# Six more blocks of layer 0's output projection folded to 448 rows, and the oT moves of layer 2 issued in five groups

## The chip, the cores and the metric

The kernel runs on one core of a Trainium2 chip. TensorE (PE in the profile) multiplies; VectorE (DVE) and ScalarE (ACT) do the elementwise work, empty the PSUM banks and normalise; SyncE (SP) issues nearly all the DMAs, in one queue and in program order; GpSimd (POOL) only fills a few tiles at the start. The metric is the device time of one execution in microseconds, the median of several runs.

## The reference

Four layers in a row on x of 2048 tokens x 448 values, in bfloat16. Layers 0 and 2 are windowed attention with 16 heads of 28 values, layers 1 and 3 a gated unit (GLU) with an inner width of 1792. The two attention layers have the same weights, and so have the two GLU layers.

```python
def _A_ref(x, wqkv, wo):          # H = 16, Dh = 28, W = 8, dil = 2
    ...
    idx = pos[:, None] - off[None, :]      # the token itself and 7 before it, two apart
    ...
    logits = jnp.einsum("bhsd,bhswd->bhsw", q, kg) * scale
    ...
    attn = _softmax(logits, axis=-1)
    o = jnp.einsum("bhsw,bhswd->bhsd", attn, vg)
    return o.transpose(0, 2, 1, 3).reshape(B, S, D) @ wo

def _B_ref(x, w_gate, w_up, w_down):
    h = (x @ w_gate) * (x @ w_up)
    return h @ w_down

x = A_x
x = x + _A_ref(_layernorm(x), A_wqkv, A_wo)
x = x + _B_ref(_layernorm(x), B_w_gate, B_w_up, B_w_down)
x = x + _A_ref(_layernorm(x), A_wqkv, A_wo)
x = x + _B_ref(_layernorm(x), B_w_gate, B_w_up, B_w_down)
```

What the change touches is the last step of `_A_ref`, the product of the attention's output o with wo.

## The kernel before

Tokens are tiled in 16 blocks of 128 (NBLK); x stays in SBUF as x_sb for the whole program. A layer is worked off in chunks of 256 or 512 tokens, and chunks of all four layers overlap in time, as dependencies allow.

Attention, for a chunk: bn_stats and xn (L583 to L604) normalise blocks of x; DMA transposes on SP (L607) turn xn_sb into xnTa; TensorE makes Q, K (WQK) and V (WV) from it. V is taken through a tile vt by plain DMAs (L723) and turned back by DMA transposes (L734) into v_sb, in windows of keys. The 17 query tiles (the first of 128 tokens, the others of 120; "query tile" 0 alone, then 1 and 2, 3 and 4 and so on as groups) go through a scores product (L837), exp and mask (L847, L854), and a weighted sum of V (L872) on 64*32 tiles of TensorE. L886 and L890 gather the sum in O_sb, L900 to L902 take the reciprocal of the softmax's denominator (a shuffle on VectorE, Ln and Exp on ScalarE), and the norm product L913 writes oT, the attention's output with head rows down the partitions.

oT has four chunks of 128 partitions: 4 groups of 32 rows, of which 28 are a head's values and 4 are padding. It is a ring over half of the tokens: 1024 columns. The output projection of two blocks B and B + 1 (`y_blocks`, key Y) multiplies oT's columns by wo_g, which is wo laid out in the same rows. TensorE works on 64 rows at a time with two such matmuls side by side (`twin_blocks`, `pair`, L352; L355 where a matmul is cut in four strips of 32 columns because it stands amid small-tile work). Unfolded that is 4 chunks x 2 halves x 2 blocks, 16 matmuls of 64 rows by 448 columns. Folded it is 14, for 448 rows instead of 512: the upper 64 rows of chunk 3 hold two heads, and four DMAs on SP (mv, L445, `oT<-oT`) copy these into the padding rows of the other chunks (table PADS: 3 or 4 rows deep, from and to the rows it names). The two blocks' lower halves of chunk 3 must then run side by side, so a fifth DMA (mw) copies the odd block's half from partitions 0 to 63 to 64 to 127; it waits for the four, and the projection waits for it. wo_g is brought into the same form by four DMAs from DRAM and one inside SBUF (wf, `wo_g<-in_A_wo_dram`, `wo_g<-wo_g`), once, after the last unfolded projection.

FOLD tells from which block on a layer is folded; `{0: 16, 2: 0}` is none in layer 0 and all in layer 2. There each pair of blocks has its own five moves: 8 x 5 = 40.

GLU, for a chunk: xn and transposes to xnTb, gate and up products (WGU, two PSUM banks side by side), g_sb from one bank by ScalarE (L979), hT = g_sb x the other bank by VectorE (L982), then the down product (WD). The last blocks' down product is at L994.

The order of all this isn't left to a queue at run time. Operations are given numbers, and tables ORDER (one list per engine) and BANKS (which PSUM bank a TensorE operation writes) fix what follows what on each engine; "538+539+556*349" in the TensorE list interleaves small-tile work with the wide matmuls. A semaphore wait is placed where an operation needs another engine's result. SP's list is an order of issue: a DMA whose data isn't ready holds all that stand behind it on SP. The tables were made by a search off line, with a model of durations.

Of the kernel before, what the change touches and what calls it, by code (L numbers as in the profile page):

```python
# [33 lines left out]
FOLD = {0: 16, 2: 0}  # L34
# [62 lines left out]
def grp_nc(g):  # L97
# [22 lines left out]
    ),  # L120
    "act": (
# [1003 lines left out]
```

## Time and profile before

| | us |
|---|---|
| runs | 381.83, 383.13, 384.85 |
| median | 383.13 |
| profiled execution | 383.47 |
| its span | 381.7 |

The rows of the page and the trace that the prediction uses are quoted there. How to read them: a row of the timeline has the start in us, the duration, the engine, the line, the operation, the tile written and the tiles read, the shape and how many instructions are put together; a bracket at the end tells how long the engine stood idle ahead of it and what ended that. "64*128" is the part of TensorE's array that a matmul uses, rows by columns; two of 64*128 run side by side. SPq is SP's queue: the time in which DMAs were being issued there, not the time of the transfers. An order's row, further down, has the line, the operation and the shape of the write's tile, and `x16` is that many in a row. Line numbers are one higher after the change up to L900, and three higher near the end.

### The profile page before, as it was taken

To read this page: it belongs to the slowest core of one execution; us is meant where nothing else is said; L and a number is where in the kernel's file an instruction comes from. 1 tells how busy PE (TensorE), PEld (TensorE's weight loads), DVE (VectorE), ACT (ScalarE), POOL (GpSimd) and SP (SyncE) were. 2 spreads that over 40 slices of the span, in tenths; PEclk is the share of its full clock that TensorE was granted. 3 is DMA by queue.
4 is the path that set the end of the run, shared out by engine and by line. 5 is a ranking of instruction groups with operands and counts; after the bars stand their busy time and mean duration, and the time that the engine had idled before them with its cause. 6 is when DMAs were issued, how large, how long until landed. Compare 5 with 4: busy or idle time off the path is not lost.

```text
span 381.7 us, 14424 instructions
## 1 busy us (share of the span) xinstructions
PE 373.9 (98%) x6388; PEld 209.8 (55%) x6388; DVE 288.1 (75%) x649; ACT 198.0 (52%) x379; POOL 7.8 (2%) x36
## 2 busy tenths in 40 slices
PE   7999999999999999999999999999989999999997
PEld 3645577654554445444676666555555544444864
DVE  7988999989759794968568977758887878266423
ACT  5798896766516355245645326628745633034410
POOL 7000000000000000000000000000000000000000
PEclk9999999999999999999999999999999999999999
DMA  7665543500130215332102221630124001502003
GB/s 262 165 158 147 96 127 81 97 7 3 26 78 16 43 25 72 43 43 44 34 18 27 45 50 29 106 47 6 25 43 76 9 19 29 122 17 47 2 2 120
DMA packets 56209, 22.97 MB, mean 60 GB/s; under 512 B 45812, under 2 KB 56132, under 8 KB 56148
## 3 DMA queue, kind: packets, MB, share of 16 engines
q1 hardware_dynamic: 56004, 22.00, 27.5%
q8 instruction: 50, 0.82, 0.9%
q14 instruction: 11, 0.09, 0.1%
q10 hardware_dynamic: 144, 0.06, 0.1%
HBM read 8.59 MB, written 2.71 MB: 30 GB/s over the span
## 4 chain that ended last, share of the span: by engine, by line
PE 91%; DVE 4%; ACT 2%; DMA 1%; issue 1%; SPq 0%; DVEq 0%
PE ps L352 82%; PE ps L355 4%; PE ps L837 2%; PE ps L872 2%; PE ps L994 1%; ACT qk L714 1%; DMA v_sb<-vt 1%; DVE xn_sb L604 1%; DVE st L583 1%; DMA x_sb<-in_A_x_dram 1%; DVE v_sb L806 0%; DVE WQK L522 0%; DVE hT L982 0%; DVE Qz L825 0%; DVE xnTa L628 0%
## 5 line engine op out<-in xcount | busy, mean ns | idle before, releaser
L352 PE MATMUL ps<-xnTb,WGU 64*128 64x512 bf16 (+1 forms) x1890 | 171.2, 332 | 0.3 <-DVE qk L714 0.3
L352 PEld LDWEIGHTS ps<-xnTb,WGU 64*128 64x128 bf16 x1890 | 92.3, 94 | 70.6 <-issue 1.6
L979 ACT ACTIVATE g_sb<-ps 128x512 bf16<-128x512 f32 (+1 forms) x140 | 69.3, 510 | 83.9 <-PE ps L352 72.0
L982 DVE TENSOR_TENSOR hT<-g_sb,ps 128x512 bf16<-128x512 bf16 (+1 forms) x140 | 78.0, 574 | 36.3 <-ACT g_sb L979 35.5
L352 PE MATMUL ps<-WD,hT 64*128 64x448 bf16 x794 | 81.3, 349 | 0.0
L352 PEld LDWEIGHTS ps<-WD,hT 64*128 64x128 bf16 x794 | 38.3, 94 | 33.3 <-ACT E_sb L847 0.4
L943 DVE TENSOR_TENSOR x_sb<-x_sb,ps 128x448 bf16<-128x448 bf16 x62 | 37.1, 613 | 21.6 <-PE ps L352 21.3
L352 PE MATMUL ps<-xnTa,WQK 64*128 64x512 bf16 (+1 forms) x490 | 51.8, 352 | 0.3 <-DVE WQK L522 0.2
L847 ACT ACTIVATE E_sb<-ps,shift_sb 128x1024 bf16<-128x1024 f32 (+1 forms) x36 | 37.5, 1072 | 12.0 <-PE ps L837 11.9
L583 DVE BATCH_NORM_STATS2 st<-x_sb 128x6 f32<-128x448 bf16 x64 | 38.3, 613 | 1.0 <-DMA x_sb<-in_A_x_dram 0.8
L604 DVE TENSOR_SCALAR xn_sb<-x_sb,mv,rstd 128x512 bf16<-128x512 bf16 (+1 forms) x64 | 35.4, 574 | 2.5 <-ACT rstd L588 2.0
L352 PEld LDWEIGHTS ps<-xnTa,WQK 64*128 64x128 bf16 x490 | 23.0, 94 | 20.7 <-DVE O_sb L890 0.4
L714 ACT ACTIVATE qk<-ps 128x1024 bf16<-128x1024 f32 (+1 forms) x29 | 26.6, 931 | 11.4 <-PE ps L352 6.3
L901 ACT ACTIVATE R_sb<-R_sb 128x480 f32<-128x480 f32 (+1 forms) x34 | 20.4, 604 | 17.2 <-DVE R_sb L900 17.0
L854 DVE TENSOR_TENSOR E_sb<-E_sb,MK 128x1024 bf16<-128x1024 bf16 (+1 forms) x36 | 23.5, 656 | 6.6 <-ACT E_sb L847 6.6
L352 PE MATMUL ps<-wo_g,oT 64*128 64x448 bf16 x236 | 27.1, 349 | 1.1 <-DVE hT L982 1.1
L913 DVE TENSOR_TENSOR oT<-O_sb,R_sb 128x480 bf16<-128x480 f32 (+3 forms) x36 | 21.9, 626 | 3.8 <-ACT R_sb L902 3.6
L352 PE MATMUL ps<-WV,xnTa 64*128 64x336 bf16 (+3 forms) x248 | 23.2, 304 | 0.5 <-DVE O_sb L890 0.5
L900 DVE STREAM_SHUFFLE R_sb<-O_sb 128x480 f32<-128x480 f32 (+1 forms) x34 | 23.1, 692 | 0.0
L586 ACT ACTIVATE lnv<-mv,eps_sb 128x2 f32<-128x2 f32 (+2 forms) x31 | 9.0, 295 | 25.9 <-DVE mv L585 24.0
L902 ACT ACTIVATE R_sb<-R_sb 128x480 f32<-128x480 f32 (+1 forms) x34 | 20.0, 607 | 0.3
L886 ACT ACTIVATE O_sb<-ps 128x512 f32<-128x512 f32 (+1 forms) x20 | 10.9, 570 | 15.8 <-PE ps L872 15.8
(66 smaller groups left out, 223.8 us busy)
## 6 DMA issues: line engine op xcount, KB each, us to landing
out_dram<-x_sb SPq DMA_DIRECT2D x15, 112.0 KB, 1.8
x_sb<-in_A_x_dram SPq DMA_DIRECT2D x3, 448.0 KB, 5.3
hT<-in_A_wqkv_dram SPq DMA_DIRECT2D x4, 224.0 KB, 4.4
WGU<-in_B_w_gate_dram SPq DMA_DIRECT2D x4, 224.0 KB, 3.9
WGU<-in_B_w_up_dram SPq DMA_DIRECT2D x4, 224.0 KB, 4.5
WD<-in_B_w_down_dram SPq DMA_DIRECT2D x2, 448.0 KB, 3.8
WGU<-in_B_w_gate_dram SPq DMA_DIRECT2D x2, 336.0 KB, 4.5
WGU<-in_B_w_up_dram SPq DMA_DIRECT2D x2, 336.0 KB, 4.8
```

The costliest lines, as they stand in the source:

```text
L352: return lambda E: E.matmul(out(), lhs(), rhs(), start=start, stop=stop)
L583: sc.add("dve", one(lambda E, B=B: E.bn_stats(st6[:, B, :], x_sb[:, B, :]), ("bn", li, B)), 525.0, deps=[("x", li - 1, B)] + ([("xn", li - ...
L604: sc.add("dve", one(lambda E, B=B, dst=dst, src=src: E.tensor_scalar(dst, src, mv[:, B, 0:1], rstd[:, B:B + 1], ALU.subtract, ALU.mult), ( ...
L714: return E.activation(dst, src, ACT.Copy) if hasattr(E, "activation") else E.tensor_copy(dst, src)
L847: return E.activation(E_sb[:, slot, 2 * hp:2 * hp + 2, 0:w], ps[:, b0:b0 + 2, 0:w], ACT.Exp, bias=shift_sb[:, 0:1], scale=SCALE)
L854: return E.tensor_tensor(e, e, MK[:, kind, 0:nc].unsqueeze(1).unsqueeze(1).to_broadcast([128, 2, w // nc, nc]), ALU.min)
L900: sc.add("dve", one(lambda E: E.stream_shuffle(R_sb[:, rs, 0:w], O_sb[:, os_, 0:w], [DH] * 32), ("Rs", li, qb)), dve_est(w) + 20.0, deps=[ ...
L901: sc.add("act", one(lambda E: E.activation(R_sb[:, rs, 0:w], R_sb[:, rs, 0:w], ACT.Ln), ("Rl", li, qb)), act_est(w, False), deps=[("Rs", l ...
L913: return E.tensor_tensor(oT[:, :, a % HALF:a % HALF + z - a], O[:, :, a - tok:z - tok], R_sb[:, rs, 0:w].rearrange("p (h n) -> p h n", h=4 ...
L943: sc.add("dve", one(lambda E: E.tensor_tensor(x_sb[:, B, :], x_sb[:, B, :], ps[:, bk[w], 0:D], ALU.add), ("x", li, B)), dve_est(D), deps=[ ...
L979: sc.add("act", one(lambda E, gs=gs, bk=bk: E.activation(g_sb[:, gs, 0:nt], ps[:, bk[0], 0:nt], ACT.Copy), ("G", li, j, fc)), act_est(nt), ...
L982: sc.add("dve", one(lambda E, gs=gs, bk=bk, fc=fc: E.tensor_tensor(hT[:, fc, hs, 0:nt], g_sb[:, gs, 0:nt], ps[:, bk[1], 0:nt], ALU.mult), ...
```

## The change

1. FOLD[0] goes from 16 to 10: layer 0's blocks 10 to 15, three pairs, are folded as well. The wf moves of the weights come after layer 0's projection of blocks 8 and 9 now, not after that of 14 and 15. Layer 0 has 3 x 5 moves of oT of its own.
2. GROUPS: in layer 0 each folded pair has its own five moves; in layer 2 there are five groups of blocks, 0 to 1, 2 to 5, 6 to 9, 10 to 13 and 14 to 15, with one set of five moves for each: 25. A set waits for the norms of all the group's blocks, and every projection of the group waits for its mw. The number of moves in all stays 40, and SP has 220 DMAs before and after.
3. The ring oT is shifted by 256 columns, so that a group's columns lie together; the norm product is cut where the ring wraps, at tokens 768 and 1792 instead of at 1024 (one instruction more in each attention layer).
4. ORDER and BANKS are new, for all engines.

```diff
-FOLD = {0: 16, 2: 0}
+FOLD = {0: 10, 2: 0}
+GROUPS = {0: tuple(range(0, 16, 2)), 2: (0, 2, 6, 10, 14)}
...
 ORDER = {
     "pe": (
-        "47 48 49 50 51 52 53 54 55 112 56 57 58 109 59 60 61 127 62 130 206 238 207 136 239 133 194 198 195 199 232 200 233 196 201 226 197 227 228 155 149 229 "
+        "47 48 49 50 51 52 53 54 55 112 56 57 58 59 109 60 61 62 206 130 127 207 238 133 136 239 198 194 232 195 233 196 200 199 197 201 228 226 155 149 227 229 "
...
-        cut = [tok] + [HALF] * (tok < HALF < tok + nq) + [tok + nq]
+        cut = [tok] + [e for e in range(HALF - 256, S, HALF) if tok < e < tok + nq] + [tok + nq]
...
-                return E.tensor_tensor(oT[:, :, a % HALF:a % HALF + z - a], ...
+                return E.tensor_tensor(oT[:, :, (a + 256) % HALF:(a + 256) % HALF + z - a], ...
...
     def y_blocks(li, B, prio):
         bk = Banks(2)
-        nd = []
-        for qb in range(NQB):
-            _, _, tok, nq = qb_info(qb)
-            if tok < 128 * (B + 2) and tok + nq > 128 * B:
-                nd.append(("N", li, qb))
+        def norms(b0, b1):
+            return [("N", li, qb) for qb in range(NQB) if qb_info(qb)[2] < 128 * b1 and qb_info(qb)[2] + qb_info(qb)[3] > 128 * b0]
+        nd = norms(B, B + 2)
         fold = B >= FOLD[li]
         if fold:
-            a = 128 * (B % 8)
-            for j, row, m, _, _ in PADS:
-                plain_dma("sp", oT[32 * j + DH:32 * j + 32, 0:m, a:a + 256], oT[row:row + 4 * m, 3, a:a + 256], ("mv", li, B, j), f"d_m{li}_{B}", deps=nd, prio=prio - 0.1)
-            plain_dma("sp", oT[64:128, 3, a + 128:a + 256], oT[0:64, 3, a + 128:a + 256], ("mw", li, B), f"d_m{li}_{B}", deps=[("mv", li, B, j) for j in range(4)], prio=prio - 0.1, mode=1)
-            nd = nd + [("mw", li, B)]
+            G = max(g for g in GROUPS[li] if g <= B)
+            n = min([g for g in GROUPS[li] if g > B] + [NBLK]) - G
+            if B == G:
+                a = 128 * ((B + 2) % 8)
+                for j, row, m, _, _ in PADS:
+                    plain_dma("sp", oT[32 * j + DH:32 * j + 32, 0:m, a:a + 128 * n], oT[row:row + 4 * m, 3, a:a + 128 * n], ("mv", li, B, j), f"d_m{li}_{B}", deps=norms(B, B + n), prio=prio - 0.1)
+                odd = [oT[lo:lo + 64, 3, a:a + 128 * n].rearrange("p (b w) -> p b w", w=256)[:, :, 128:256] for lo in (64, 0)]
+                plain_dma("sp", odd[0], odd[1], ("mw", li, B), f"d_m{li}_{B}", deps=[("mv", li, B, j) for j in range(4)], prio=prio - 0.1, mode=1)
+            nd = nd + [("mw", li, G)]
```

What the new tables do at the places of which the prediction speaks:

On TensorE, from the last weighted sum (L872, L873 after) of layer 2's query tiles 5 and 6 to the first projections from oT. WD,hT is layer 1's down product, xnTb,WGU with 256 columns the gate and up products of layer 3's first chunk. Before, the first wo_g rows are blocks 2 and 3, the second ones blocks 4 and 5:

```order
L872 MATMUL ps<-E_sb,v_sb 32x64 x16
L352 MATMUL ps<-WD,hT 128x448 x58
L352 MATMUL ps<-xnTb,WGU 128x256 x56
L352 MATMUL ps<-WD,hT 128x448 x28
L352 MATMUL ps<-xnTb,WGU 128x256 x14
L352 MATMUL ps<-wo_g,oT 128x448 x8
L352 MATMUL ps<-xnTb,WGU 128x256 x14
L352 MATMUL ps<-wo_g,oT 128x448 x6
L352 MATMUL ps<-WD,hT 128x448 x14
L352 MATMUL ps<-xnTb,WGU 128x256 x28
L352 MATMUL ps<-WD,hT 128x448 x14
L352 MATMUL ps<-wo_g,oT 128x448 x8
```

After, with the first wo_g rows those of blocks 4 and 5:

```order
L873 MATMUL ps<-E_sb,v_sb 32x64 x24
L353 MATMUL ps<-WD,hT 128x448 x10
L353 MATMUL ps<-xnTb,WGU 128x256 x14
L353 MATMUL ps<-WD,hT 128x448 x42
L353 MATMUL ps<-xnTb,WGU 128x256 x14
L353 MATMUL ps<-WD,hT 128x448 x42
L353 MATMUL ps<-xnTb,WGU 128x256 x42
L353 MATMUL ps<-WD,hT 128x448 x14
L353 MATMUL ps<-wo_g,oT 128x448 x8
L353 MATMUL ps<-xnTb,WGU 128x256 x14
```

Blocks 4 and 5 have moved ahead of blocks 2 and 3, with less TensorE work between them and the weighted sum.

On VectorE, the same stretch: from the add L890 (L891 after) that closes the sum of query tiles 5 and 6 to the norm products L913 (L914) of these two. Before:

```order
L890 TENSOR_TENSOR O_sb<-O_sb,ps 128x2x4x8
L913 TENSOR_TENSOR oT<-O_sb,R_sb 128x4x120
L604 TENSOR_SCALAR xn_sb<-x_sb,mv,rstd 128x512 x2
L943 TENSOR_TENSOR x_sb<-x_sb,ps 128x448
L913 TENSOR_TENSOR oT<-O_sb,R_sb 128x4x120
L943 TENSOR_TENSOR x_sb<-x_sb,ps 128x448
L583 BN_STATS st<-x_sb 128x6
L900 STREAM_SHUFFLE R_sb<-O_sb 128x480 x2
L943 TENSOR_TENSOR x_sb<-x_sb,ps 128x448
L583 BN_STATS st<-x_sb 128x6
L982 TENSOR_TENSOR hT<-g_sb,ps 128x256
L585 BN_AGGR mv<-st 128x2
```

Four more rows (an hT, an aggregate) come ahead of the two norms there. After:

```order
L891 TENSOR_TENSOR O_sb<-O_sb,ps 128x2x4x8
L901 STREAM_SHUFFLE R_sb<-O_sb 128x480
L605 TENSOR_SCALAR xn_sb<-x_sb,mv,rstd 128x512
L901 STREAM_SHUFFLE R_sb<-O_sb 128x480
L985 TENSOR_TENSOR hT<-g_sb,ps 128x256 x2
L914 TENSOR_TENSOR oT<-O_sb,R_sb 128x4x120
L946 TENSOR_TENSOR x_sb<-x_sb,ps 128x448 x2
L914 TENSOR_TENSOR oT<-O_sb,R_sb 128x4x40
L914 TENSOR_TENSOR oT<-O_sb,R_sb 128x4x80
```

The shuffles and norms of the two tiles have moved ahead of most x adds and statistics; the second norm is in two pieces, of 40 and 80 tokens.

On SP, layer 2's first transposes of V (L734, L735 after) and what stands ahead of and among them; xnTa is layer 2's second chunk, xnTb layer 1's fourth. Before:

```order
L723 DMA vt<-qk 4x4x512 x4
L607 DMA_TRANSPOSE xnTb<-xn_sb 128x7x128 x2
L723 DMA vt<-qk 4x4x512 x2
L734 DMA_TRANSPOSE v_sb<-vt 128x128 x2
L607 DMA_TRANSPOSE xnTa<-xn_sb 128x4x128
L445 DMA wo_g<-in_A_wo_dram 4x1792
L734 DMA_TRANSPOSE v_sb<-vt 128x128
L607 DMA_TRANSPOSE xnTa<-xn_sb 128x4x128 x3
```

After, where `oT<-oT` are moves of layer 0's blocks 14 and 15:

```order
L446 DMA oT<-oT 4x4x256
L724 DMA vt<-qk 4x4x512 x4
L446 DMA oT<-oT 64x128
L608 DMA_TRANSPOSE xnTb<-xn_sb 128x7x128
L724 DMA vt<-qk 4x4x512 x2
L608 DMA_TRANSPOSE xnTb<-xn_sb 128x7x128 x2
L735 DMA_TRANSPOSE v_sb<-vt 128x128 x3
L608 DMA_TRANSPOSE xnTa<-xn_sb 128x4x128 x4
L735 DMA_TRANSPOSE v_sb<-vt 128x128
```

The first three transposes of V have come together, the weight move is gone from among them, and two moves of layer 0 stand among the copies to vt ahead of them.

On SP in layer 0, the transposes xnTb of layer 1's third chunk and what stands around them (before, the first xnTb row belongs to the second chunk). Before:

```order
L723 DMA vt<-qk 4x4x256
L607 DMA_TRANSPOSE xnTb<-xn_sb 128x7x128
L734 DMA_TRANSPOSE v_sb<-vt 128x128 x3
L607 DMA_TRANSPOSE xnTb<-xn_sb 128x7x128 x3
L734 DMA_TRANSPOSE v_sb<-vt 128x128
L607 DMA_TRANSPOSE xnTb<-xn_sb 128x7x128
```

After, where `wo_g<-in_A_wo_dram` are the weight moves and `oT<-oT` those of layer 0's blocks 10 and 11:

```order
L446 DMA wo_g<-in_A_wo_dram 4x1792
L735 DMA_TRANSPOSE v_sb<-vt 128x128
L446 DMA oT<-oT 4x4x256
L446 DMA wo_g<-in_A_wo_dram 4x1792
L446 DMA oT<-oT 4x3x256
L608 DMA_TRANSPOSE xnTb<-xn_sb 128x7x128
L446 DMA oT<-oT 4x3x256
L608 DMA_TRANSPOSE xnTb<-xn_sb 128x7x128
L446 DMA oT<-oT 4x4x256
L608 DMA_TRANSPOSE xnTb<-xn_sb 128x7x128 x2
```

The transposes have come behind two moves and between two more, and behind the weight moves.

More of the change, by code (lines that the diff above doesn't have):

```diff
@@ L105 @@
     "pe": (
[14 rows of a table removed]
[14 rows of a table added]
     ),
     "act": (
[12 rows of a table removed]
[12 rows of a table added]
     ),
     "dve": (
[18 rows of a table removed]
[18 rows of a table added]
     ),
     "pool": (
-        "21 24 25 32 26 23 35 39 33 36 18 34 28 44 20 37 29 40 19 30 38 27 41 31 42 43 22 67 64 71 78 73"
+        "24 18 28 29 25 39 40 32 33 35 41 26 20 22 21 30 27 36 19 31 34 42 37 43 44 68 66 38 77 23 76"
     ),
     "sp": (
[7 rows of a table removed]
[7 rows of a table added]
     ),
@@ L912, in fn @@
             def fn(E, a=a, z=z):
-                return E.tensor_tensor(oT[:, :, a % HALF:a % HALF + z - a], O[:, :, a - tok:z - tok], R_sb[:, rs, 0:w].rearrange("p (h n) -> p h n", h=4)[:, :, a - tok:z - tok], ALU.mult)
+                return E.tensor_tensor(oT[:, :, (a + 256) % HALF:(a + 256) % HALF + z - a], O[:, :, a - tok:z - tok], R_sb[:, rs, 0:w].rearrange("p (h n) -> p h n", h=4)[:, :, a - tok:z - tok], ALU.mult)
             ins.append((fn, ("N", li, qb) if z == cut[-1] else None))
@@ L936, in y_blocks @@
             nd = nd + [("wf", 4)]
-        twin_blocks(lambda w: ps[:, bk[w], 0:D], lambda w, c, lo: oT[lo:lo + 64, c, 128 * ((B + w) % 8):128 * ((B + w) % 8) + 128], lambda w, c, lo: wo_g[lo:lo + 64, c, :],
+        twin_blocks(lambda w: ps[:, bk[w], 0:D], lambda w, c, lo: oT[lo:lo + 64, c, 128 * ((B + w + 2) % 8):128 * ((B + w + 2) % 8) + 128], lambda w, c, lo: wo_g[lo:lo + 64, c, :],
                     (("Y", li, B), ("Y", li, B + 1)), [range(4)], [[]], nd + WO, prio, bk, short=int(fold))
```

130 rows, old and new, of tables (BANKS, ORDER) are left out of this document.

## The prediction, made before the change was run

> **What bounds the kernel now.** I read the page first: busy time and the chain that ended last. Then the waits of TensorE, and last the timelines of TensorE, VectorE and SyncE's DMA queue around each place that the change touches.
>
> ```profile
> PE 373.9 (98%) x6388; PEld 209.8 (55%) x6388; DVE 288.1 (75%) x649; ACT 198.0 (52%) x379; POOL 7.8 (2%) x36
> PE 91%; DVE 4%; ACT 2%; DMA 1%; issue 1%; SPq 0%; DVEq 0%
> ```
>
> TensorE is busy for 98% of the span, and 91% of the chain is its own work. So a matmul less is time less, a TensorE wait is time more, and other work counts only where TensorE stands still for it. It stands still in few places (engine, line waited for, us in total, times, longest):
>
> ```profile
> PE ps L514 <- DVE hT L475: 1.3, 1, 1.3
> PE ps L352 <- DVE hT L982: 1.1, 1, 1.1
> PE ps L614 <- DVE xn_sb L604: 0.7, 2, 0.4
> PE ps L872 <- DMA v_sb<-vt: 0.5, 1, 0.5
> PE ps L352 <- DVE O_sb L890: 0.5, 1, 0.5
> ```
>
> The first and third belong to the start of the program. The second and fourth lie where the change rewrites the DMA queue, and they carry half of my sum.
>
> **Term 1: six blocks of layer 0 folded, -0.57.** A projection of two blocks takes 16 matmuls unfolded and 14 folded. Folded ones run in layer 2 already (start, duration, count at the end):
>
> ```profile
> 224.11 1.49 PE L352 MATMUL ps<-WD,hT 64*128 64x448 bf16 x14
> 225.43 0.92 PE L352 MATMUL ps<-wo_g,oT 64*128 64x448 bf16 x8
> 226.19 0.93 PE L352 MATMUL ps<-xnTb,WGU 64*128 64x256 bf16 x14
> 226.95 0.73 PE L352 MATMUL ps<-wo_g,oT 64*128 64x448 bf16 x6
> 227.52 0.93 PE L352 MATMUL ps<-xnTb,WGU 64*128 64x256 bf16 x14
> ```
>
> By the starts, 8 such matmuls take 0.76 and 6 take 0.57: two cost 0.19. Three pairs of blocks lose two each: 0.57, all on TensorE's own path. The price is on the DMA queue, where 15 issues for layer 0 are added and 15 for layer 2 fall away; TensorE pays only if something behind them comes late.
>
> **Term 2: the wait at 277.1 goes, -1.14.** In the timelines of TensorE, VectorE and SyncE's queue:
>
> ```profile
> 275.95 1.16 PE L352 MATMUL ps<-WV,xnTa 64*128 64x336 bf16 x14
> 278.25 0.93 PE L352 MATMUL ps<-wo_g,oT 64*128 64x448 bf16 x8 [1.14 <-DVE hT L982]
> ```
>
> ```profile
> 269.28 0.66 DVE L913 TENSOR_TENSOR oT<-O_sb,R_sb 128x480 bf16<-128x480 f32 x1
> 274.62 1.14 DVE L943 TENSOR_TENSOR x_sb<-x_sb,ps 128x448 bf16<-128x448 bf16 x2
> ```
>
> ```profile
> 269.97 2.69 SPq L445 DMA_DIRECT2D oT<-oT  x4
> 274.73 0.54 SPq L445 DMA_DIRECT2D oT<-oT  x1
> ```
>
> This is the projection of layer 2's blocks 8 and 9. The releaser named, the GLU product, is not read by it. What it reads from VectorE was done at 269.94, and its banks were free at 275.76. What is left is the fifth move (oT, lower half to upper), issued at 274.73. After the change one set of five moves serves blocks 6 to 9, and the wait for its fifth move falls to the projection of blocks 6 and 7, priced in term 5. Blocks 8 and 9 follow with nothing of their own to wait for. I take the whole 1.14; the ends are 0 (the same lateness shows in the next row) and 1.14.
>
> **Term 3: the wait at 162.3 goes, -0.53.** Layer 2's first weighted sum waits there for a transpose of V:
>
> ```profile
> 155.17 4.70 PE L352 MATMUL ps<-xnTb,WGU 64*128 64x512 bf16 x42
> 159.70 1.49 PE L352 MATMUL ps<-WD,hT 64*128 64x448 bf16 x14
> 162.82 0.25 PE L872 MATMUL ps<-E_sb,v_sb 64*32 64x64 bf16 x16 [0.53 <-DMA v_sb<-vt]
> ```
>
> ```profile
> 157.47 1.26 SPq L607 DMA_TRANSPOSE xnTa<-xn_sb  x1
> 158.83 0.42 SPq L445 DMA_DIRECT2D wo_g<-in_A_wo_dram  x1
> 159.30 2.36 SPq L734 DMA_TRANSPOSE v_sb<-vt  x1
> ```
>
> Between the second and the third transpose of V stand an xnTa transpose and a weight move, 1.26 + 0.42 = 1.68 us of the queue. In the new order the weight moves are back in layer 0 and the three transposes follow each other. What is new ahead of them, a fourth and a fifth move of layer 0's blocks 14 and 15, costs the queue two issues (1.2 us) and what the fifth still waits for the four, at most the 2.0 seen in term 5 less four copies to vt between. TensorE also has more to do first: by the order, its work between the last QK product of that chunk and this sum grows from 17.5 to 20.3 us, at the prices of the rows (42 matmuls 512 wide in 159.70 - 155.17 = 4.53). 1.7 less and 1.2 more on the queue against 2.8 more of cover: 0.53 is gone with some 2 us to spare. The ends are 0 and 0.53; I take all.
>
> **Term 4: one more change of tile size, +0.23.** Small-tile bursts (64*32) stand between the large ones, and counted in the order of instructions TensorE changes tile size 81 times before and 83 after.
>
> ```profile
> 117.62 0.59 PE L352 MATMUL ps<-xnTb,WGU 64*128 64x512 bf16 x4
> 118.14 0.28 PE L872 MATMUL ps<-E_sb,v_sb 64*32 64x64 bf16 x24
> ...
> 118.46 0.24 PE L872 MATMUL ps<-E_sb,v_sb 64*32 64x64 bf16 x16
> ...
> 118.73 0.33 PE L872 MATMUL ps<-E_sb,v_sb 64*32 64x64 bf16 x24
> 118.99 0.39 PE L352 MATMUL ps<-xnTb,WGU 64*128 64x512 bf16 x2
> ```
>
> On the way in, 4 matmuls at 4.53 / 42 = 0.108 should take 0.43 and 0.52 pass: 0.09. On the way out, 24 small ones take 0.26. With 8 wide strips beside them, 24 took 0.32 and 16 took 0.27, so 8 cost 0.05 and 24 cost 0.13: the rest is 0.13. The pair costs 0.22 to 0.23; the ends are 0 (the new burst may be one already split by a weight change) and twice that.
>
> The Trainium skill speaks against this step: the page "TensorEngine Tiling (Array Packing)", under Key Properties, says that changing the tiling mode needs a drain. If a drain costs the part of a large matmul's duration that normally overlaps the next (the last row's two, side by side, last 0.39, and two take 0.22 in a run: 0.17 each way), the pair would be 0.34 and the sum 0.1 higher. The stretch above shows less.
>
> **Term 5: the new groups of layer 2, +0.1.** The first group is blocks 0 and 1 as before. For blocks 2 to 5 there is now one set of moves, which waits for the norms of block 5, and TensorE first uses it at blocks 4 and 5.
>
> ```profile
> 206.99 0.28 PE L872 MATMUL ps<-E_sb,v_sb 64*32 64x64 bf16 x16
> 208.73 0.22 DVE L890 TENSOR_TENSOR O_sb<-O_sb,ps 128x64 f32<-128x64 f32 x1
> 213.15 0.70 DVE L900 STREAM_SHUFFLE R_sb<-O_sb 128x480 f32<-128x480 f32 x1
> 216.37 1.33 DVE L913 TENSOR_TENSOR oT<-O_sb,R_sb 128x480 bf16<-128x480 f32 x2 [0.25 <-ACT R_sb L902]
> 213.47 6.24 SPq L445 DMA_DIRECT2D oT<-oT  x7
> 221.00 2.55 SPq L445 DMA_DIRECT2D oT<-oT  x2
> ```
>
> Before, the last weighted sum of these blocks ended at 207.27, their norms at 217.70 (10.4 later), and the fifth move for blocks 4 and 5 was issued at 223.0 (the second issue of the last row, 0.54 long) for matmuls at 225.43, with no wait: 18.2 us of TensorE work lay between. After, by the order, it is 108 matmuls 448 wide (1.32 for 14, so 10.2) and 70 of 256 (0.77 for 14, so 3.85): 14.0. If the norms kept their 10.4, the moves would be late. But VectorE's order brings the last norm from 17 to 9 places behind the add of 208.73 that closes the weighted sum. That add ends 1.7 after the sum; two shuffles with one xn between them follow it at once in the new order (about 0.65 each: 3.6 after the sum), and the norms began 2.5 after the last shuffle's end before. I estimate the norms done at 6.1 to 6.6. Four moves 0.67 apart (the 2.69 of term 2), then the fifth 2.0 after the issue of the fourth (223.0 - 221.00), is 4.0 to 4.3; the fifth is usable 2.4 us after its issue (225.43 - 223.0). That makes 12.5 to 13.3 against 14.0: hidden, with under 2 us to spare. The moves carry twice the bytes, a form that no row of before shows; the ends of this cost are 0 and 3.9 (norms as late as before, and the last move landing 3.5 after its issue, as the one of 274.73 did for 278.25: 10.4 + 4.0 + 3.5 = 17.9 against 14.0). Behind the fifth move stand three xnTa transposes, which the chunk's QK products need some 20 us after the weighted sum: safe unless the moves are late too.
>
> For blocks 6 to 9 the work between is 18.9 us before by the timeline, less 14 matmuls of 448 (1.3) plus 8 of 336 (0.6): 18.2. The chain is norms 10.5, four moves among V's moves 4.3, landing 2.4 to 3.5: 17.2 to 18.3. That is the +0.1.
>
> **Term 6: layer 0's queue, 0.** The added moves and the weight moves stand ahead of four xnTb transposes that feed layer 1's third chunk:
>
> ```profile
> 104.26 0.65 DVE L913 TENSOR_TENSOR oT<-O_sb,R_sb 128x480 bf16<-128x480 f32 x1
> 102.11 4.70 SPq L607 DMA_TRANSPOSE xnTb<-xn_sb  x3
> 113.95 2.32 PE L352 MATMUL ps<-xnTb,WGU 64*128 64x512 bf16 x20
> ```
>
> The first added move waits for the norm of 104.26 and would hold the transposes of 102.11. In the new order that norm stands ahead of four GLU products that came before it, and of three of these transposes' four xn, at about 98 by my estimate from TensorE's rows between, so four issues of 0.7 lie in front of transposes that were issued from 102.11 on, for matmuls that come near 112. I take 0; the ends are 0 and 2 (the norm as late as before). Two more norm pieces on VectorE (75% busy) and the start of the program, whose order is changed in a few rows, I cost at nothing, give or take 0.3: VectorE's idle quarter hides them.
>
> **Sum.** -0.57 - 1.14 - 0.53 + 0.23 + 0.1 = -1.9. The profiled execution took 383.47 (span 381.7 and 1.77 around it), 0.34 above the median of the three runs, 383.13. So 381.6 for a profiled execution, and 381.2 to 381.6 for a median; I say 381.5.
>
> **Rivals.** (a) Only the fold counts; the waits wander: with all orders searched anew, two waits like those of 1.14 and 0.53 appear in other rows, since every transfer that lands late still has a TensorE row behind it. For it: the five waits above total 4.1 us and sit in five unlike places. Then 383.13 - 0.57 + 0.23 = 382.8. (b) The other side: the moves of blocks 2 to 5 are late. Its place is the first projection of blocks 4 and 5; its price 2.8 to 3.9; it decides once the chain passes 14.0 + 1.9 = 15.9 us, that is norms later than about 9 us after the weighted sum. For it: 18.2 us of cover became 14.0, and before the norms came at 10.4. Against it: VectorE's new order. Then 381.5 + 3.4 = 384.9, slower than before. (c) More goes than I count: the start and the small waits in the same order (0.5 + 0.5 + 0.3) go too: 380.0.
>
> **How the numbers follow.** Forecast 0.54, (a) 0.22, (b) 0.15, (c) 0.09. The forecast's own range is 380.6 to 382.4: terms 4 to 6 off by up to half a microsecond each way, and the gap of 0.34 between profile and median. The range 379.8 to 384.4 takes in (a), (c) down to a little below its 380.0, and (b) at its lowest price (381.5 + 2.8 = 384.3); it leaves out the rest of (b), about 0.1, and the tail of (c). About 1% is what a measurement of this kernel tells from no change, the three runs lying 0.8% apart: faster by over 1% (below 379.3) needs (c) and more, 0.07; slower by over 1% (above 387.0) needs (b) at its upper end with the three transposes behind it or layer 0's queue late too, 0.04; within 1% is the rest, 0.89.
>
> **What would show it.** Term 1: six wo_g matmuls fewer, and TensorE's work lower by it. Term 2: no wait over 0.3 at the projections of blocks 6 to 9. Term 3: no row "DMA v_sb<-vt" among the waits. Term 5: the last norm of blocks 2 to 5 within 7 us of the weighted sum's end and no wait at blocks 4 and 5; a wait of 2 us or more there means that (b) is right. Term 6: no idle time before the first matmuls of layer 1's third chunk. The prediction falls if waits total over 4 us again in other rows, or if TensorE's work itself, by the starts in undisturbed stretches, has grown.

## The result, and the profile after

| | before | after |
|---|---|---|
| median of 13 runs, us | 383.25 | 380.42 |
| lowest to highest | 381.83 to 384.85 | 380.05 to 382.32 |
| profiled execution (its span) | 383.47 (381.7) | 380.47 (378.7) |

The ratio is 0.9927, 95% interval 0.9911 to 0.9944: 0.7% faster, 2.8 us, where 1.6 to 1.9 were forecast. Beside the median the spread has changed: 12 of the 13 runs after lie between 380.05 and 381.09, while those before fill 3 us.

The page of the kernel after, busy time and the chain:

```profile
PE 373.6 (99%) x6376; PEld 208.7 (55%) x6376; DVE 285.4 (75%) x647; ACT 200.0 (53%) x384; POOL 7.8 (2%) x35
...
PE 96%; ACT 2%; POOL 1%; DVE 1%; issue 0%; DVEq 0%; POOLq 0%
```

TensorE's waits of the kernel after:

```profile
PE ps L515 <- DVE hT L476: 1.3, 1, 1.3
PE ps L615 <- POOL ident L482: 0.3, 1, 0.3
PE ps L838 <- ACT qk L715: 0.3, 1, 0.3
PE ps L353 <- DVE O_sb L891: 0.2, 1, 0.2
```

The chain held 1% DMA and 4% VectorE before; the DMAs are gone from it. Of the waits only the first, at the start of the program, is left as it was, and none is for a DMA.

To see where the time went I take, for each matmul, its start less the array's own time for all matmuls before it: their columns, each counted by the share of the array that the matmul uses, at 2.4 columns of the full array a nanosecond. That pace is a yardstick, chosen a little above the one of the undisturbed rows (42 matmuls of 512 columns on half the array in 4.53 us, by the rows of term 3, are 2.37), so about 1% of the work done, 4 us by the end, is counted as lost in both. The difference is TensorE's lost time, and two traces can be compared at the same amount of work done:

| work done, us | 48 | 144 | 152 | 248 | 256 | 288 | 344 |
|---|---|---|---|---|---|---|---|
| lost before | 11.15 | 15.98 | 17.19 | 21.41 | 23.34 | 25.13 | 25.85 |
| lost after | 10.95 | 15.96 | 16.29 | 20.61 | 21.08 | 22.61 | 23.42 |
| difference | -0.20 | -0.03 | -0.90 | -0.79 | -2.26 | -2.52 | -2.42 |

The two spans differ by 3.0: 0.56 is work (352.98 against 352.42) and 2.4 is lost time. The two large steps, -0.9 and -1.5, are the waits of terms 3 and 2. By the starts they are larger than the profile's brackets say: by the same yardstick the matmul at 162.82 came 0.71 after the work ahead of it was through the array, not 0.53, and the one at 278.25 came 1.31 after it, not 1.14, because the bracket begins at the modelled end of the last matmul, which overlaps the next one's start. A wait "by the starts" is meant in this way from here on.

### The profile page after: what moved, and what is told of

Read it like the earlier page. It is cut to its first block, busy times and chain, and to the rows that moved or that the text cites. A ratio compares the mean times of both kernels' runs of the same rounds, so it can differ in the third digit from the quotient of the medians.

```text
span 378.7 us, 14371 instructions
## 1 busy us (share of the span) xinstructions
PE 373.6 (99%) x6376; PEld 208.7 (55%) x6376; DVE 285.4 (75%) x647; ACT 200.0 (53%) x384; POOL 7.8 (2%) x35
## 4 chain that ended last, share of the span: by engine, by line
PE 96%; ACT 2%; POOL 1%; DVE 1%; issue 0%; DVEq 0%; POOLq 0%
PE ps L353 86%; PE ps L356 4%; PE ps L838 2%; PE ps L873 2%; PE ps L997 1%; POOL hT L493 1%; ACT E_sb L848 1%; PE ps L619 0%; PE ps L515 0%; ACT xnTa L626 0%; ACT qk L715 0%; DVE Qz L826 0%; PE ps L615 0%; ACT v_sb L807 0%; ACT xnTa L629 0%
## 5 line engine op out<-in xcount | busy, mean ns | idle before, releaser
L353 PE MATMUL ps<-xnTb,WGU 64*128 64x512 bf16 (+1 forms) x1898 | 173.3, 332 | 0.0
L353 PEld LDWEIGHTS ps<-WD,hT 64*128 64x128 bf16 x786 | 37.4, 94 | 32.4 <-DVE hT L985 0.2
L605 DVE TENSOR_SCALAR xn_sb<-x_sb,mv,rstd 128x896 bf16<-128x896 bf16 (+1 forms) x64 | 35.0, 568 | 6.6 <-ACT rstd L589 5.8
L715 ACT ACTIVATE qk<-ps 128x1024 bf16<-128x1024 f32 (+1 forms) x28 | 25.4, 931 | 14.2 <-PE ps L353 12.0
L914 DVE TENSOR_TENSOR oT<-O_sb,R_sb 128x480 bf16<-128x480 f32 (+5 forms) x38 | 22.2, 600 | 5.3 <-ACT R_sb L903 5.3
L353 PE MATMUL ps<-wo_g,oT 64*128 64x448 bf16 x228 | 25.6, 349 | 0.0
L826 DVE TENSOR_SCALAR Qz<-qk,qmask 128x960 bf16<-128x960 bf16 (+1 forms) x36 | 14.7, 451 | 7.5 <-ACT qk L715 6.5
```

The costliest lines, as they stand in the source:

```text
L353: return lambda E: E.matmul(out(), lhs(), rhs(), start=start, stop=stop)
L605: sc.add("dve", one(lambda E, B=B, dst=dst, src=src: E.tensor_scalar(dst, src, mv[:, B, 0:1], rstd[:, B:B + 1], ALU.subtract, ALU.mult), ( ...
L715: return E.activation(dst, src, ACT.Copy) if hasattr(E, "activation") else E.tensor_copy(dst, src)
L914: return E.tensor_tensor(oT[:, :, (a + 256) % HALF:(a + 256) % HALF + z - a], O[:, :, a - tok:z - tok], R_sb[:, rs, 0:w].rearrange("p (h n ...
```

## The experiments

### Two DMAs of the old order moved (e1, e2, e3)

The rows of SP's order that change in the kernel before. First e1, then e2; e3 has both:

```diff
 oT<-oT 4x3x256          (the four moves of blocks 8 and 9)
+oT<-oT 64x128           (their fifth)
 v_sb<-vt 128x128
 vt<-qk 4x4x512 x2
-oT<-oT 64x128
```

```diff
 v_sb<-vt 128x128 x2
+v_sb<-vt 128x128
 xnTa<-xn_sb 128x4x128
 wo_g<-in_A_wo_dram 4x1792
-v_sb<-vt 128x128
```

> The kernel before, with one DMA moved on SP: the fifth move of layer 2's blocks 8 and 9 comes directly behind their four moves, ahead of a transpose of V and two copies to vt. My theory (the wait of 1.14 at 277.1 is for this move): it is issued when the last of the four has landed, about 2.0 after its issue at 272.0, so at 274.0 instead of 274.73, and TensorE's wait before the first matmul of blocks 8 and 9 gets 0.7 shorter: about 382.5. Rival (the wait is for the GLU product that the profile names): the wait stays 1.1 and the time 383.2.

> The kernel before, with one DMA moved on SP: layer 2's third transpose of V comes directly behind the second, ahead of an xnTa transpose and a weight move. My theory: it is issued 1.7 earlier, so the wait of 0.53 at 162.3 is gone and the span is shorter by 0.5 to 0.7: about 382.6. Rival (the waits wander): the wait goes and another of the same size comes behind it, since the xnTa transpose is now 1.2 later: 383.2.

> The kernel before with both DMAs moved on SP, the fifth move and the third transpose of V. My theory: the two gains add, 0.7 + 0.6 = 1.3 off: about 381.9, which is nearly half of the 2.8 that the change brings. Rival (waits wander): less than the larger of the two.

Against the kernel before on the same chip (median 382.57): e1 383.1, ratio 1.0009 (0.9993 to 1.0025); e2 382.29, 0.9990 (0.9974 to 1.0006); e3 382.61, 1.0012 (0.9998 to 1.0026). No gain in any. The traces explain half of it. The timeline of TensorE in e1 at blocks 8 and 9, and its waits:

```profile
275.11 1.16 PE L353 MATMUL ps<-WV,xnTa 64*128 64x336 bf16 x14
276.10 0.92 PE L353 MATMUL ps<-wo_g,oT 64*128 64x448 bf16 x8
```

```profile
PE ps L353 <- DMA xnTb<-xn_sb: 0.8, 1, 0.8
PE ps L873 <- DMA v_sb<-vt: 0.8, 1, 0.8
```

The wait before the wo_g matmuls is gone, all of it and not the 0.7 that I expected, so it was for the fifth move and not for the GLU product. In e2, where that place is as before, the profile even names it:

```profile
277.17 0.93 PE L353 MATMUL ps<-wo_g,oT 64*128 64x448 bf16 x8 [0.67 <-DMA oT<-oT]
```

In e1 SP now stands for 1.3 us until the four moves have landed, with the transposes of V behind it, and two new waits of 0.8 come (at 280 and 294, by the starts 0.98 and 1.01). In e3 the traced execution has neither the old waits nor new ones (0.3 by the starts at 280, span 379.9). SP's queue from the moves to the four transposes of V, first e1, then e3:

```profile
269.13 4.48 SPq L446 DMA_DIRECT2D oT<-oT  x5
...
278.22 5.68 SPq L735 DMA_TRANSPOSE v_sb<-vt  x4
```

```profile
269.16 4.47 SPq L446 DMA_DIRECT2D oT<-oT  x5
...
277.57 5.50 SPq L735 DMA_TRANSPOSE v_sb<-vt  x4
```

The order and the issues are the same there to within 0.05 us up to the copies to vt (274.95); only the transposes that follow come 0.65 later in e1. So the move's 1.3 us on SP takes room away, but it isn't the whole cause of e1's new wait at 280: the same order of this stretch had next to none in another execution. The traced execution of e3 took 381.63, the lowest of its 12 runs (381.63 to 384.45); the usual one is 1 us slower, and no trace shows where.

### The kernel before once more (c1)

> The kernel before, unchanged, for a second trace of it. The theory formed from the runs so far: the two waits of terms 2 and 3 are no fixed property of the old order; transposes land up to 1 us later in one execution than in another, and the old order has places where that reaches TensorE. Then this trace loses the same time as the first (within 0.2) outside of a few waits, and the waits for V's transpose at about 162 and for the moves at about 277 differ in size from 0.71 and 1.31 by some tenths or more, or others stand in their place. Rival (the two waits are fixed): 0.71 and 1.31 again, within 0.1.

One run, 384.4, span 382.7. The timeline of TensorE at the two places, and a third:

```profile
49.66 1.05 PE L352 MATMUL ps<-xnTb,WGU 64*128 64x256 bf16 x16 [1.03 <-DVE R_sb L900]
...
163.22 0.25 PE L872 MATMUL ps<-E_sb,v_sb 64*32 64x64 bf16 x16 [0.61 <-DMA v_sb<-vt]
...
279.19 0.93 PE L352 MATMUL ps<-wo_g,oT 64*128 64x448 bf16 x8 [1.24 <-DVE hT L982]
```

By the starts the two are 0.80 and 1.40, 0.09 more each than in the first trace: the rival's outcome. In the same execution a third place lost 1.22 where it had lost 0.51, and a wait of 0.50 for xnTb stood at 244 that was not there before. So both is true: the two waits recur in the old order, and others come and go by up to 0.7. In e1 the wait at 162 was missing, with the order there untouched: its transpose of V landed 2.64 after its issue began and not 3.48 as in the first trace (2.23 in c1, where it was issued 1.6 later). The difference is in the issue on SP, which took 1.53 there, 2.36 in the first trace and 1.12 in c1; from its end to the landing it is 1.1 in all three.

### All DMAs late, in both orders (c3, c4)

```diff
+    for n, i in enumerate(LATE):
+        plain_dma("sp", late[:, n, :], A_wo[0:64, 0:8], ("late", n), "d_late", deps=list(sc.ops[i].deps))
```

LATE holds 68 DMAs, the same by name in both kernels; each extra one stands directly ahead of its DMA in SP's list.

> The kernel before, with 68 small extra DMAs on SP (64 rows of 16 bytes, into a tile that nobody reads), each directly ahead of one DMA and waiting for the same as it: ahead of all transposes of x in layers 1 (from block 2) to 3, of V in layer 2, and of the fifth moves of blocks 0, 2, 6, 10 and 14. Each DMA so treated comes about 0.3 to 0.5 later, and those in a run of four up to 2 later. My theory: the old order has no room for that in several places, so this kernel loses 3 to 6 us against itself: 386 to 389. Rival (the new order isn't more tolerant, only better at two places): the same loss as the kernel after has with the same extra DMAs.

> The kernel after, with the same 68 extra DMAs ahead of the same named DMAs. My theory: the new order has room for most of it: 0.5 to 2 us lost, 381 to 382.5, and so 2 to 4 us less lost than the kernel before loses. Rival (not more tolerant): it loses what the kernel before loses, within 1 us.

On one chip, with the kernel before at 382.73: c3 414.97, ratio 1.0822 (1.0757 to 1.0886), c4 390.58, ratio 1.0208 (1.0170 to 1.0246). Against itself the old order loses 8.2%, 32 us, and the new one 2.8% (1.0208 / 0.9927), 10 to 11 us. Both sizes are far over my numbers. I had an extra DMA at 0.3 to 0.5; over the 68, SP's queue in c4 has a median of 0.59 for its issue and 0.63 to the next one's start. One of them:

```profile
162.76 0.60 SPq L451 DMA_DIRECT2D late<-in_A_wo_dram  x1
163.41 1.26 SPq L613 DMA_TRANSPOSE xnTa<-xn_sb  x1
```

TensorE's largest waits in c3, and then in c4 (whose traced execution was its slowest, 395.03, the other four being 390.4 to 390.7):

```profile
PE ps L357 <- DMA xnTb<-xn_sb: 11.4, 6, 4.7
PE ps L877 <- DMA v_sb<-vt: 8.0, 5, 3.5
...
PE ps L357 <- DMA xnTa<-xn_sb: 0.9, 1, 0.9
```

```profile
PE ps L358 <- DMA xnTb<-xn_sb: 3.6, 4, 2.5
PE ps L358 <- DMA xnTa<-xn_sb: 3.2, 3, 1.9
...
PE ps L878 <- DMA v_sb<-vt: 0.8, 2, 0.5
```

The direction is plain: with the same lateness, the old order waits 20.3 us for transposes and the new one 7.6, in its slowest execution. The new order is the more tolerant one, by a factor of 3 in time lost. Not all of the loss is waiting: the granted clock of TensorE was 0.50 for 20.5 us of c3's traced execution and for 3.4 us of c4's (mean 0.975 and 0.996), which comes on top of the waits.

### The parts alone, in the old order (e8, e9)

```diff
-FOLD = {0: 16, 2: 0}
+FOLD = {0: 10, 2: 0}     (e8; e9 has the GROUPS and the shifted ring, and FOLD as before)
```

> The kernel before with FOLD[0] = 10 and nothing else of the change: pairs in layer 2, TensorE's, VectorE's and ScalarE's old orders; SP gets layer 0's 15 moves put in as early as their norms allow without holding transposes that are due, and the weight moves after blocks 8 and 9. My theory: the fold's 0.57 on TensorE is paid only if its moves are hidden, and the old order doesn't hide them: blocks 10 and 11 are due at 108.5, their norms end at 106.1, and four moves, a fifth and a landing take 6.6, so a wait of about 4 to 5; the same at blocks 12 and 13 (due 125.0, norms 124.0, so about 5, less what the first wait gives); next to nothing at 14 and 15. In all +8, about 391. Rival (the fold alone is the gain, the order only tidies up): 382.7.

> The kernel before with the five groups in layer 2 and the shifted ring, layer 0 unfolded, all orders old; a group's moves stand where the first pair's stood. My theory: the groups need the new order. The group of blocks 2 to 5 waits for the norms that ended at 217.7, and its fifth move is usable 6.6 later, 224.3, while TensorE wants blocks 2 and 3 at 219.2: a wait of 5. The group of blocks 6 to 9 waits for 269.9, usable at 276.5 to 277.6, wanted at 272.3: 4 to 5, and the wait before blocks 8 and 9 is gone. In all +8, about 391, or more since four copies to vt and transposes stand behind the moves on SP. Rival (the groups by themselves save queue time and so time): 382 or less.

e8 took 398.47, ratio 1.0420 (1.0394 to 1.0445), and e9 396.12, ratio 1.0353 (1.0303 to 1.0404): 16 and 13 us slower, and 7 and 5 over my estimates. The waits of e8 and of e9:

```profile
PE ps L353 <- DMA oT<-oT: 5.3, 2, 4.1
PE ps L353 <- issue: 4.6, 1, 4.6
PE ps L353 <- DMA xnTb<-xn_sb: 1.7, 1, 1.7
```

```profile
PE ps L353 <- issue: 6.2, 1, 6.2
PE ps L353 <- DMA oT<-oT: 3.8, 1, 3.8
```

The large ones stand where they were expected, before blocks 10 and 11 and 12 and 13 in e8, 2 and 3 and 6 and 7 in e9, and their sizes are about right ("issue" is the wait for the fifth move here too; the row behind it is the first wo_g matmul of blocks 2 and 3). In e8 three more came that I had at next to nothing or not at all: 1.1 at blocks 14 and 15, 1.7 for xnTb, 1.1 for a transpose of V. What I had left out in both is what a long wait does to the matmuls after it. The windows of e9 around its first wait (columns: window, length, busy time of each engine, granted clock, DMA):

```profile
218.00:224.00 6.00, 0.44 (x9) 0.14 (x4) 0.72 (x2) 0.38 (x1) 0.00 (x0) 0.80 0.15 35
224.00:226.00 2.00, 1.38 (x8) 0.69 (x10) 0.00 (x0) 0.00 (x0) 0.00 (x0) 0.50 0.44 90
226.00:228.00 2.00, 2.00 (x20) 1.48 (x18) 0.00 (x0) 0.00 (x0) 0.00 (x0) 0.50 0.60 121
...
230.00:232.00 2.00, 2.00 (x38) 1.77 (x34) 1.54 (x4) 0.83 (x3) 0.00 (x0) 1.00 0.00 0
```

For 3.8 us after the wait the granted clock is 0.50. In lost time this place cost 8.2: 6.35 of standing still and 1.8 of running slowly. The second wait (3.9 by the starts) was followed by 6.2 us at 0.50 and cost 6.8 in all. Both runs tell of the parts with the moves put where they were put; another place for them in the old order was not tried.

### The parts undone in the new order (e4, e5)

```diff
-                    (...), [range(4)], [[]], nd + WO, prio, bk, short=int(fold))
+                    (...), [range(4)], [[]], nd + WO, prio, bk, short=int(fold and li == 2))
```

```diff
-GROUPS = {0: tuple(range(0, 16, 2)), 2: (0, 2, 6, 10, 14)}
+GROUPS = {0: tuple(range(0, 16, 2)), 2: tuple(range(0, 16, 2))}
```

> The kernel after, with the last six blocks of layer 0 multiplied in 16 matmuls instead of 14; all moves, orders and waits stay. The two heads in the upper half of chunk 3 are thereby added twice for these blocks. It isolates term 1: my price is 0.19 for a pair of blocks, 0.57 for the three, so 381.0, and in the trace TensorE's ideal work up by 0.56 with its lost time unchanged. Rival (two matmuls less are swallowed by waits elsewhere): no difference from 380.4.

> The kernel after with layer 2's moves in pairs again: 15 DMAs more on SP, each pair's moves put where the group's stood, those of the pair that TensorE uses first ahead, and the two fifth moves behind all eight. My theory: the groups as such save only SP's time; the fifth move for blocks 4 and 5 comes about 1.1 later (four issues more of 0.67, less the 1.6 that SP stood waiting), within the slack of 1.3 that the trace after has there; the one for blocks 6 and 7 likewise: 380.4 to 381.0. Rival (the grouping is what took the time off, since SP's queue was too full): waits come back at blocks 4 and 5 or 6 and 7 or at what stands behind them on SP, 382 or more.

e4: 380.96, ratio 0.9952 (0.9938 to 0.9966). e5: 380.95, ratio 0.9948 (0.9934 to 0.9962). Each is 0.5 above the kernel after by the medians; against the kernel before that ran beside them (382.82, not the 383.25 of the table) it is 1.0 and 0.8 by the ratios. Each interval overlaps that of the kernel after (0.9911 to 0.9944). The trace tells more. In e4 the array's work is 352.98, 0.56 more than after, and no wait has gone for it. Lost time is 0.6 lower at 32 us of work (7.40 against 7.98, all of it from the start of the program) and 0.3 lower at 296 (22.45 against 22.72), which is why the span (379.1) is only 0.3 longer. The fold's 0.56 of work is there, and the 0.5 to 1.0 between the runs fits it, though the intervals alone would not show it. In e5 no wait came back at the groups' places; the only new one is 0.40 for xnTa at 223, behind the added moves on SP. The groups by themselves are worth 0.5 to 0.8 us at most in this order; the span of the trace is 0.2 longer.

### One fifth move late (e6)

```diff
-oT<-oT 64x2x128         (the fifth move of blocks 2 to 5)
 xnTa<-xn_sb 128x4x128 x3
+oT<-oT 64x2x128
```

> The kernel after, with the fifth move of blocks 2 to 5 put behind the three xnTa transposes that followed it, on SP. It tests how near rival (b) of the prediction was. My theory: the move is issued at about 217.2 instead of 214.5, is usable 2.4 to 3.5 later, and TensorE, due at 218.2, waits 1.4 to 2.5 at blocks 4 and 5: 381.8 to 382.9. If the slack there is larger than I think, no wait and 380.4.

384.99, ratio 1.0053 (1.0034 to 1.0071): 4.6 above the kernel after by the medians, 4.8 by the ratios, where 1.4 to 2.5 were expected. SP's queue and then TensorE in e6:

```profile
209.82 2.69 SPq L447 DMA_DIRECT2D oT<-oT  x4
212.55 6.83 SPq L609 DMA_TRANSPOSE xnTa<-xn_sb  x3
219.43 0.70 SPq L447 DMA_DIRECT2D oT<-oT  x1
```

```profile
221.52 1.68 PE L354 MATMUL ps<-wo_g,oT 64*128 64x448 bf16 x8 [3.53 <-issue]
222.96 1.73 PE L354 MATMUL ps<-xnTb,WGU 64*128 64x256 bf16 x14
224.46 0.82 PE L354 MATMUL ps<-wo_g,oT 64*128 64x448 bf16 x6
```

The three transposes took 6.83 of SP's time and not 3.8, since the second had to wait for its xn; the move came at 219.43 and was used 2.1 later. TensorE stood for 3.7 by the starts, and then ran at half speed: 8 wo_g matmuls took 1.44 (222.96 - 221.52) where they take 0.76. Not every execution did: two of the four (385.33, the traced one, and 385.65) have a mean granted clock of 0.996, the other two (384.16 and 384.65) one of 1.000, and they are 1.1 us faster in the mean.

### Ten bursts split (e7)

Tables' rows of TensorE; the first of ten, where two sums (625, 626) shared a burst beside one wide product (472) and now stand beside one each:

```diff
-625+626*472/4/3 469
+625*472/2/5 626*469/2/3
```

> The kernel after, with ten small-tile bursts of two operations each split in two, so that large matmuls stand between: 20 more changes of tile size, ten more pairs, with the same matmuls and the same number of them cut in strips. It measures term 4. By the rows before, 0.22 to 0.23 for a pair: +2.2 to 2.3, so 382.7. By the drain as the Trainium skill's tiling page would have it with the durations, 0.34 for a pair: +3.4, 383.8. If a change of tile size costs nothing that wasn't there before: 380.4.

386.29, ratio 1.0087 (1.0072 to 1.0101), 5.9 above the kernel after. Most of that is waits that the splits made (1.32, 0.79, 0.56, 0.50 and four smaller, 4.1 by the starts: scores and sums now come later for ScalarE and VectorE). What the tile changes cost stands apart. The trace has 103 changes of tile size where the kernel after has 83; those with a gap of under 0.14 us by the starts are 94 against 74, and their gaps are 2.14 more in all: 0.21 a pair over ten pairs. One split place:

```profile
107.48 0.21 PE L874 MATMUL ps<-E_sb,v_sb 64*32 64x64 bf16 x8
107.63 0.74 PE L354 MATMUL ps<-WD,hT 64*128 64x448 bf16 x6
108.30 0.22 PE L874 MATMUL ps<-E_sb,v_sb 64*32 64x64 bf16 x8
```

Six wide matmuls at 0.094 take 0.57 and 0.67 pass; eight small ones at 0.05 end in 0.15: 0.10 each way. The Trainium skill's page "TensorEngine Tiling (Array Packing)", Key Properties, that a change of tiling mode drains the TensorE, is borne out in kind, as time is lost at each change; the reading that a drain costs the whole overlap of a matmul's duration, 0.34 a pair, is not.

## Why the prediction came out as it did

Direction, range and the place of the large terms were right; the gain was 2.8 where 1.6 to 1.9 were forecast, and part of the hit is luck, as terms 2, 3 and 5 and rival (c) show. Step by step:

- **Term 1, the fold (-0.57):** right. The work fell by 0.56 by the matmuls of the trace, and e4 gave it back.
- **Terms 2 and 3, the waits at 277.1 and 162.3 (-1.14 and -0.53):** both went, and the first was for the fifth move, as argued against the name in the profile (e1, e2). Mis-sized: the brackets' 1.67 is 2.02 by the starts (0.71 + 1.31). And the reason was too narrow. Two queue positions in the old order, put right, remove both waits from a trace (e3) and nothing from the median, so -1.67 was not there to be had at these two places alone. What the new order has is more room at its transfers: 10 to 11 us lost against 32 when the same 68 DMAs are late. That also fits the smaller spread of its runs, but that this room is what took off the rest is argued, not shown. At the place of term 3 the room is larger than the 2 us that I gave it. In the timelines of SP and TensorE of the kernel after, the last of the three transposes of V ends its issue at 153.6 and lands at 154.8, 4.2 us ahead of the sum; before, it landed at 162.77 for the sum of 162.82:

```profile
149.07 4.57 SPq L735 DMA_TRANSPOSE v_sb<-vt  x3
```

```profile
159.02 0.25 PE L873 MATMUL ps<-E_sb,v_sb 64*32 64x64 bf16 x16
```

- **Term 4, the tile changes (+0.23):** the price was right (0.21 in e7; by the prediction's own rows it is 0.20, since 8 small ones at 0.05 make 24 cost 0.15 and not 0.13), but it was not paid. The traces have the 81 and 83 changes that I counted, yet those with a gap of under 0.14 us by the starts are 74 in both, and their gaps come to 8.01 before and 7.97 after. Counting changes in the order did not tell how many of them would leave such a gap.
- **Term 5, the groups (+0.1):** 0. The mechanism was as described: the weighted sum ended at 204.2, and in the timelines of VectorE and SP the last norm ended 6.0 later (6.1 to 6.6 forecast); the fifth move, the last of the row of five, began at 214.52. The matmuls of blocks 4 and 5 ran without a wait:

```profile
209.47 0.72 DVE L914 TENSOR_TENSOR oT<-O_sb,R_sb 128x160 bf16<-128x160 f32 x2
```

```profile
210.22 4.99 SPq L446 DMA_DIRECT2D oT<-oT  x5
```

```profile
216.90 1.49 PE L353 MATMUL ps<-WD,hT 64*128 64x448 bf16 x14
218.22 0.92 PE L353 MATMUL ps<-wo_g,oT 64*128 64x448 bf16 x8
```

With 2.1 from issue to use (e6), 1.6 us were to spare there. Blocks 6 to 9 had a fifth move at 271.01 for matmuls at 274.61 and no wait either. There the sum rests on norms 10.5 after the weighted sum, for which the prediction shows no row: in the trace before it is 11.8 (258.18 to 269.94), which with the same moves would have meant a wait of up to 1.4, and after it is 9.6 (256.67 to 266.24). So this part came out by VectorE's new order, which the prediction works out for blocks 2 to 5 alone.

- **Term 6, layer 0's queue (0):** right. The norm that I placed at about 98 ended at 98.9, the last of the four transposes was issued at 107.6, and the matmuls followed at 112.7 with no idle time.
- **The rest:** -0.2 at the start of the program and -0.3 between 256 and 288 us of work were in no term. At the start the traces of one and the same program differ by up to 0.4, so the first tells nothing.
- **Rivals:** (a), that waits wander, is not what the change did. In the old order e1 did it, and e2 a little (a new 0.36 at 243), while in c1 both waits came again. (b) didn't come; e6, with a wait of 3.7, shows that I had priced it too low at 3.4: its four runs are 3.7 to 5.2 above the kernel after, and the two upper ones ran part of the way at half speed. (c), more than I counted, is nearest by the number, 380.0 against 380.42 (by its own 1.3 off 381.5 it would be 380.2), but not by its reason: the start and its small waits gave 0.2 (by 48 us of work) and not 1.3.

Open: in which waits an ordinary execution of e3 loses the 1 us that its traced one did not have, and so how the 2.3 us beside the fold divide between the two known waits and the rest. Shown is that the parts cost 13 to 16 us in the old order with the moves placed as in e8 and e9, that the runs with either undone in the new one are 0.5 to 1.0 slower (with intervals that overlap the one of the kernel after), and that the new order bears late DMAs better.

## What to carry to other kernels

Where one engine is busy for 98%, a wait for a DMA in one trace is a sample: before it is put down to a place, take a second trace, and before a queue position is moved, look at what stands behind it, since SP's waiting takes room away there. What an order loses when many of its transfers are made a little late told these two orders apart better than the waits in one trace did. And a change that lengthens a chain (moves that wait for four blocks, a fold that needs transfers) is to be made together with the order that gives it room; alone it cost many times what it saved here.

## What was not expected of the hardware

- **The clock after a wait.** In the traces of e6, e8, e9, c3 and c4 the granted clock fell to 0.50 amid the program, for stretches of 3.41 or 6.83 us, and full clock was back 2.7 to 6.2 us after TensorE had gone on. That cost 1.5 us on top of a wait of 3.7 (e6), 1.8 on top of 6.35 and 2.9 on top of 3.9 (both e9). It came with waits of 2.3 us (c3) and 2.5 us (c4) too, and with none of 1.9 us (the next longest, in c4) or less; in e6 it came in two executions of four. The Trainium skill's page "TensorE: Matmul & The Clock Gate", Part 1, has half the clock after an idle window of about 3.4 us and full clock after about as long of sustained work. The stretches here agree with that length, but waits that were shorter than it were enough, and the way back took up to 6.2 us.
- **The same transfer, the same program, another landing.** A transpose of V took 2.37 from issue to landing in one execution of the kernel before and 4.14 in another (c1). Of the 75 transposes, 48 agree within 0.1 us between these two traces, and 17 differ by 0.35 to 1.8. The order can't be blamed for this part of a wait, only for having no room for it.
